# A linear-attention and GEGLU block: the order of its work written by hand, and the same work ordered by a list scheduler inside the kernel

## The chip, the core and the metric

One core of a Trainium2 chip runs the kernel. Its engines each take their own queue in order: PE (TensorE, matrix products), ACT (ScalarE), DVE (VectorE), POOL (GpSimd), and SP (SyncE), which here issues every transfer between the device's memory (DRAM) and the core's working memory (SBUF). Products land in PSUM, eight banks of 128 x 512 numbers. The metric is device time in microseconds (us), the median of three runs; a profiled execution is taken beside them.

## The reference, cut to what matters

```python
x = A_x                                   # 1 x 2048 x 512, float32
xn = layernorm(x)
q, k, v = split(xn @ wqkv)                # 32 heads of 16
phi = lambda t: where(t > 0, t + 1, exp(t)) + 1e-6
kv = einsum("bhsd,bhse->bhde", phi(k), v);  z = sum over s of phi(k)
o = (phi(q) @ kv) / (phi(q) . z + 1e-6)
s = o @ wo
g = silu((gelu(xn @ w_gate) * (xn @ w_up)) @ w_down)    # w_gate, w_up: 512 x 1792
return x + s * g
```

## The kernel before

**Products.** Every large product is made of numbers split in two: a rounded high part (ACT casts it) and the rest (DVE or POOL subtracts). `mm3` (L83) issues high x high, high x low and low x high, so one product of a 128 x 256 by 256 x 512 block is six matmuls of 512 columns. The projections go by a scheme of seven block products where the plain one has eight: a 2 x 2 blocking of the activations (`xt`, and four differences `T`, made on POOL, L180) and of the weights (`tmp`, made on POOL, L376 to L379). The products carry the numbers 1 to 7 (`PRODUCTS`, L24). They gather in three PSUM tiles: X takes 1, 6, 7 and 4, one on top of the other, and is copied out by ACT after 1, 6 and 7 (`saved`, L418: `e1`, `u2`, `u3`); Y takes 2; Z takes 5 and 3. DVE adds a copy and a PSUM tile (`added`, L422) to get the four output blocks: 11 = e1 + Y, 22 = u3 + Z, 21 = X itself, 12 = u2 + Z. So a product on X has to wait until ACT has copied what stands there.

**Stages.** (A) Layer norm (`ln`, L149), transposes on PE (`transp`, L167), splits, and eight rounds (L288) over pairs of token tiles for q and k: products X, Y, Z, then exp (ACT) and sums (DVE) for phi, and `gacc` (L254), which adds xn-transposed times phi(k) into four PSUM banks `gps`. The weights wq and wk are first combined and split into seven slots `kq` (L131). q goes to DRAM (`q_d`), and so do the split activations of the first four rounds (`xh_d`, `xl_d`). (F1) The gated projection for the second half of the tokens: `ffn` (L403) runs 14 "quads" (`quad`, L447), in turn gate and up, each seven products; a gate quad ends in gelu on ACT, an up quad in a product with the gate on POOL (L438) and a split into `hh` (ACT, L441) and `hl` (DVE, L442). After units 0, 1-2 and 3-4, and at the end 5-6, `down` (L502) multiplies by w_down and adds into eight tiles `acc`. (S) The attention output: `GT`, `wv`, `wo` are loaded, `kv` and `M` made, then for each of 16 token tiles a normalisation (POOL L636, DVE L638 to L643), a transpose `ptq`, a split and twelve matmuls `sps`. (F0) `ffn` for the first half of the tokens, with the final sum in `finish` (L697).

**What sets the order.** Under `manual_schedule` (L63) the four engines run their instructions in the order in which the Python code writes them. That order is by hand: inside `quad` the products come as 2, 6, 5, 7, then 1 of the next quad, then 4 and 3; the preparation of a later quad's weights (`prep_w`, L367: four POOL sums, then casts and subtractions of four groups) is dealt out in steps, `bg` (L451), between the products. Stages have pools of their own, opened and closed one after another, and the tiles rotate through few buffers: `raw` two, `tmp` one, `w` four, X two PSUM banks, Y and Z one each.

Of the kernel before, what the change touches and what calls it, by code (L numbers as in the profile page):

```python
# [8 lines left out]
F32 = mybir.dt.float32  # L9
# [5 lines left out]
P = 128  # L15
# [10 lines left out]

@with_exitstack
def kernel(
# [21 lines left out]
    NF = F // P  # L50
    NU = NF // 2
    NP = 8

    def pool(name, bufs=1, **kw):
        return ctx.enter_context(tc.tile_pool(name=name, bufs=bufs, **kw))

    dram = pool("dram", space=bass.MemoryType.DRAM)
    cpool = pool("cpool")
    xf = pool("xf")
    wp = pool("wp")  # L60
    rawp = pool("rawp")

    ctx.enter_context(tc.manual_schedule(engines=ENGINES))  # L63

    q_d = dram.tile([S, D], F32, name="q_d")
    s_d = dram.tile([S // 2, D], F32, name="s_d")
    g_d = dram.tile([P, KT, D], F32, name="g_d")
    xh_d = dram.tile([P, 14, NC], F32, name="xh_d")
    xl_d = dram.tile([P, 14, NC], F32, name="xl_d")

    neg_half = cpool.tile([P, 1], F32, name="neg_half")
    nc.vector.memset(neg_half, -0.5)
    ones = cpool.tile([P, P], F32, name="ones")
    nc.vector.memset(ones, 1.0)
    ident = cpool.tile([P, P], F32, name="ident")
    make_identity(nc, ident)
    zacc = cpool.tile([P, D], F32, name="zacc")
    den_eps = cpool.tile([P, H], F32, name="den_eps")

    XH = xf.tile([P, 14, NC], F32R, name="XH")  # L80
    XL = xf.tile([P, 14, NC], F32R, name="XL")
# [7 lines left out]
    wqkv_k = wqkv.rearrange("(k p) n -> p k n", p=P)  # L89


    with ExitStack() as actx:
        ap = actx.enter_context(tc.tile_pool(name="ap", bufs=1))
        sm = actx.enter_context(tc.tile_pool(name="sm", bufs=2))
        psa = actx.enter_context(tc.tile_pool(name="psa", bufs=1, space=bass.MemoryType.PSUM))

        xs = {}

        def load_x(t):
            xs[t] = ap.tile([P, D], F32, name=f"x{t}", tag="x", bufs=4)  # L100
            nc.sync.dma_start(xs[t], x[t * P:(t + 1) * P, :])

        tokens = [(8 * (n // 4) + n % 4, 8 * (n // 4) + 4 + n % 4) for n in range(NP)]

        warm = psa.tile([P, P], F32, name="warm", tag="X")
        for _ in range(WARM):
            nc.tensor.matmul(warm, ones, ones, start=True, stop=True)


        wk1 = rawp.tile([P, 2, D], F32, name="wk1", tag="raw", bufs=2)  # L110
        wk2 = rawp.tile([P, 2, D], F32, name="wk2", tag="raw", bufs=2)
        wq1 = rawp.tile([P, 2, D], F32, name="wq1", tag="tmp", bufs=1)
        wq2 = ap.tile([P, 2, D], F32, name="wq2", tag="wq2")
        s1 = ap.tile([P, 2, D], F32, name="s1", tag="s1")
        load_x(0)
        nc.sync.dma_start(wk1, wqkv_k[:, 0:2, D:2 * D])
        load_x(4)
        nc.sync.dma_start(wk2, wqkv_k[:, 2:4, D:2 * D])
        nc.sync.dma_start(wq1, wqkv_k[:, 0:2, 0:D])
        nc.sync.dma_start(wq2, wqkv_k[:, 2:4, 0:D])  # L120
        load_x(1)
        load_x(5)

        KQ = [wp.tile([P, 7, D], F32R, name=f"kq{i}", tag="w", bufs=4) for i in range(4)]
        ORDER = [0, 1, 4, 3, 5, 2, 6]

        def kq(slot, lo, k):
            r = 4 * ORDER.index(slot) + 2 * lo + k
            return KQ[r // 7][:, r % 7, :]

        def kq_split(slot, raw):  # L131

            r = 4 * ORDER.index(slot)
            if r // 7 == (r + 1) // 7:
                nc.scalar.copy(KQ[r // 7][:, r % 7:r % 7 + 2, :], raw)
            else:
                for k in range(2):
                    nc.scalar.copy(kq(slot, 0, k), raw[:, k, :])
            both = (r // 7 == (r + 1) // 7) and ((r + 2) // 7 == (r + 3) // 7)
            if both:  # L140
                a, b = KQ[(r + 2) // 7], KQ[r // 7]
                nc.vector.tensor_sub(a[:, (r + 2) % 7:(r + 2) % 7 + 2, :], raw, b[:, r % 7:r % 7 + 2, :])
            else:
                for k in range(2):
                    nc.vector.tensor_sub(kq(slot, 1, k), raw[:, k, :], kq(slot, 0, k))

        lnst, xns = {}, {}

        def ln(t):  # L149
            st = sm.tile([P, 6], F32, name=f"st{t}", tag="st")  # L150
            nc.vector.bn_stats(st, xs[t])
            mv = sm.tile([P, 2], F32, name=f"mv{t}", tag="mv")
            nc.vector.bn_aggr(mv, st)
            ve = sm.tile([P, 1], F32, name=f"ve{t}", tag="ve")
            nc.vector.tensor_scalar_add(ve, mv[:, 1:2], EPS_LN)
            rstd = sm.tile([P, 1], F32, name=f"rstd{t}", tag="rstd")
            nc.gpsimd.tensor_tensor(rstd, ve, neg_half, op=ALU.pow)
            lnst[t] = mv, rstd

        def ln_norm(t):  # L160
            mv, rstd = lnst.pop(t)
            xns[t] = ap.tile([P, D], F32, name=f"xn{t}", tag="xn", bufs=5)
            nc.vector.tensor_scalar(xns[t], xs.pop(t), mv[:, 0:1], rstd, op0=ALU.subtract, op1=ALU.mult)  # L163

        xts = {}

        def transp(n, i):  # L167
            t = tokens[n][i]
            pt = psa.tile([P, KT, P], F32, name=f"pt{t}", tag="pt")
            for k in range(KT):  # L170
                nc.tensor.transpose(pt[:, k, :], xns[t][:, k * P:(k + 1) * P], ident)  # L171
            if i == 0:
                xts[n] = ap.tile([P, 2, KT, P], F32, name=f"xt{n}", tag="xt")
            nc.scalar.copy(xts[n][:, i], pt)

        Ts = {}

        def forms(n):
            xt = xts[n]
            T = Ts[n] = ap.tile([P, 4, 2, P], F32, name=f"T{n}", tag="T")  # L180
            nc.gpsimd.tensor_sub(T[:, 0], xt[:, 1, 0:2], xt[:, 0, 0:2])
            nc.gpsimd.tensor_sub(T[:, 1], xt[:, 1, 2:4], T[:, 0])
            nc.gpsimd.tensor_sub(T[:, 2], xt[:, 1, 2:4], xt[:, 1, 0:2])
            nc.gpsimd.tensor_sub(T[:, 3], xt[:, 0, 2:4], T[:, 1])

        def jsl(n):
            return slice((n % 4) * P, (n % 4 + 1) * P)

        def split_x(n, part):

            src, rows = {
                0: (xts[n][:, 0], slice(0, 4)),
                1: (xts[n][:, 1, 2:4], slice(4, 6)),
                2: (Ts[n].rearrange("p a b c -> p (a b) c") if n in Ts else None, slice(6, 14)),
            }[part]
            nc.scalar.copy(XH[:, rows, jsl(n)], src)
            nc.vector.tensor_sub(XL[:, rows, jsl(n)], src, XH[:, rows, jsl(n)])

        def spill_x(n):
            nc.sync.dma_start(xh_d[:, :, jsl(n)], XH[:, :, jsl(n)].bitcast(F32))  # L200
            nc.sync.dma_start(xl_d[:, :, jsl(n)], XL[:, :, jsl(n)].bitcast(F32))

        def prod(ps, n, i, start):
            ws, xsl = PRODUCTS[i]
            for k in range(2):
                mm3(ps, XH[:, 2 * xsl + k, jsl(n)], XL[:, 2 * xsl + k, jsl(n)],
                    kq(ws, 0, k), kq(ws, 1, k), start and k == 0, k == 1, not start)

        xn_h, xn_l, pk_h, pk_l = {}, {}, {}, {}

        def split_xn(t):
            xn = xns.pop(t)
            xn_h[t] = ap.tile([P, D], F32R, name=f"xnh{t}", tag="xnh", bufs=3)
            xn_l[t] = ap.tile([P, D], F32R, name=f"xnl{t}", tag="xnl", bufs=3)
            nc.scalar.copy(xn_h[t], xn)
            nc.gpsimd.tensor_sub(xn_l[t], xn, xn_h[t])

        def saved(ps, name):
            e = ap.tile([P, D], F32, name=name, tag="e", bufs=4)
            nc.scalar.copy(e, ps)  # L220
            return e

        def added(e, ps, name):
            c = ap.tile([P, D], F32, name=name, tag="c", bufs=3)
            nc.vector.tensor_add(c, e, ps)
            return c


        def phi_exp(v, t, nm):
            r = ap.tile([P, D], F32, name=f"{nm}r{t}", tag="r", bufs=2)  # L230
            nc.scalar.activation(r, v, AF.Relu, scale=-1.0)
            nc.scalar.activation(r, r, AF.Exp, scale=-1.0)
            return r

        def phi_add(v, r, t, nm):

            p0 = ap.tile([P, D], F32, name=f"{nm}p{t}", tag="p", bufs=4)
            nc.vector.scalar_tensor_tensor(p0, v, 0.0, r, op0=ALU.max, op1=ALU.add)
            return p0
# [496 lines left out]
```

## Time and profile before

| | |
|---|---|
| median of 3 runs | 912.86 us (907.66 to 915.66) |
| profiled execution | 914.31 us, its span from first to last instruction 912.6 us |
| busy in the span | PE 706.3 us (77%), DVE 409.3 (45%), ACT 325.4 (36%), POOL 267.1 (29%) |
| mean clock granted to PE | 0.87 of full speed |
| moved by DMA | 68.64 MB, mean 75 GB/s |

Rows of the profile give a line of the kernel, the engine, the operation, output<-input by tile names, the count (x) and busy time; "idle before" is the time the engine stood still just before, and the arrow names the instruction that ended it. PE's matmuls overlap in the pipe, so their listed durations are longer than their spacing; the spacing of their starts is what counts.

### The profile page before, as it was taken

How to read it: one execution, taken by the hardware profiler on the slowest of the kernel's cores; microseconds unless marked ns; L12 is line 12 of the kernel's file. 1: busy time of each engine (PE TensorE's matmuls, PEld its weight loads, DVE VectorE, ACT ScalarE, POOL GpSimd, SP SyncE). 2: the span in 40 equal slices, each digit the busy share in tenths (PEclk: the TensorE clock that was granted, in tenths of full speed). 3: DMA queues.
4: the chain of work that ended last, by engine and by line, in shares of the span. 5: the costliest groups of instructions: out<-in, count | busy, mean ns of one | idle time of the engine just before them, and what ended most of it. 6: DMA issues, size and time to landing. Idle time of an engine off the chain costs nothing.

```text
span 912.6 us, 7661 instructions
## 1 busy us (share of the span) xinstructions
PE 706.3 (77%) x2760; PEld 558.4 (61%) x2760; DVE 409.3 (45%) x608; ACT 325.4 (36%) x560; POOL 267.1 (29%) x277
## 2 busy tenths in 40 slices
PE   3676666697789689778979667787896897789784
PEld 2565555575667468566757545665674685667663
DVE  7655554555343443443333456553424425443333
ACT  4544454465344430333233311124443413331321
POOL 3443433344221321223112224422223212231023
PEclk7887887898789889889988788899898799799888
DMA  5433410003301110110105725323111101200024
GB/s 205 128 123 109 127 47 23 24 24 109 96 26 47 46 47 0 59 57 24 47 0 231 300 91 150 109 76 105 46 46 47 46 1 47 69 1 23 1 88 164
DMA packets 49637, 68.64 MB, mean 75 GB/s; under 512 B 2496, under 2 KB 31168, under 8 KB 49088
## 3 DMA queue, kind: packets, MB, share of 16 engines
q1 hardware_dynamic: 49600, 68.17, 22.8%
q8 instruction: 21, 0.34, 0.2%
q14 instruction: 16, 0.13, 0.0%
HBM read 49.28 MB, written 18.87 MB: 75 GB/s over the span
## 4 chain that ended last, share of the span: by engine, by line
PE 34%; DVE 13%; issue 11%; POOL 10%; ACT 9%; DMA 2%; SPq 0%; POOLq 0%; DVEq 0%; ACTq 0%
POOL c L438 6%; PE FX L85 5%; PE d L87 5%; PE d L85 5%; PE d L86 5%; PE FX L86 4%; PE FX L87 4%; DVE c L424 4%; ACT fu L419 3%; DVE w L383 2%; ACT hh L441 2%; DVE hl L442 2%; POOL u L636 1%; ACT w L382 1%; POOL tmp L377 1%
## 5 line engine op out<-in xcount | busy, mean ns | idle before, releaser
L85 PE MATMUL FX<-XH,w 128*128 128x512 f32 x224 | 111.9, 500 | 89.7 <-ACT fu L419 84.4
L438 POOL TENSOR_TENSOR c<-c,c 128x512 f32<-128x512 f32 x42 | 53.9, 1283 | 264.6 <-DVE c L424 264.6
L85 PEld LDWEIGHTS FX<-XH,w 128*128 128x128 f32 x224 | 53.7, 240 | 115.1 <-ACT fu L419 96.9
L86 PE MATMUL FX<-XL,w 128*128 128x512 f32 x224 | 105.6, 471 | 0.0
L87 PE MATMUL FX<-XH,w 128*128 128x512 f32 x224 | 104.6, 467 | 0.0
L85 PE MATMUL d<-dw,hh 128*128 128x512 f32 x224 | 87.2, 389 | 0.0
L87 PE MATMUL d<-dw,hl 128*128 128x512 f32 x224 | 87.1, 389 | 0.0
L86 PE MATMUL d<-dw,hh 128*128 128x512 f32 x224 | 87.1, 389 | 0.0
L376 POOL TENSOR_TENSOR tmp<-raw 128x256 f32<-128x256 f32 x28 | 22.1, 791 | 176.5 <-DVE w L383 176.5
L441 ACT CAST hh<-c 128x512 fp32r<-128x512 f32 x42 | 26.0, 618 | 127.9 <-POOL c L438 127.9
L442 DVE TENSOR_TENSOR hl<-c,hh 128x512 fp32r<-128x512 f32 x42 | 29.1, 692 | 94.7 <-ACT hh L441 94.7
L424 DVE TENSOR_TENSOR c<-fu,FZ 128x512 f32<-128x512 f32 x56 | 38.4, 686 | 68.9 <-ACT fu L419 51.1
L516 DVE TENSOR_TENSOR acc<-acc,d 128x512 f32<-128x512 f32 x48 | 32.9, 686 | 71.6 <-PE d L87 71.1
L87 PEld LDWEIGHTS FX<-XH,w 128*128 128x128 f32 x224 | 53.2, 237 | 13.9 <-DVE w L383 0.2
L171 PE MATMUL pt<-ident,xn 128*128 128x128 f32 x64 | 13.9, 357 | 61.6 <-DVE xn L163 61.6
L86 PEld LDWEIGHTS FX<-XL,w 128*128 128x128 f32 x224 | 54.3, 243 | 11.6
L383 DVE TENSOR_TENSOR w<-tmp,w 128x512 fp32r<-128x512 f32 x56 | 39.6, 709 | 44.7 <-ACT w L382 44.5
L419 ACT COPY fu<-FX 128x512 f32<-128x512 f32 x56 | 32.5, 581 | 56.7 <-PE FX L87 56.7
L171 PEld LDWEIGHTS pt<-ident,xn 128*128 128x128 f32 x64 | 10.1, 185 | 65.8 <-issue 61.2
L85 PE MATMUL FZ<-XH,w 128*128 128x512 f32 x112 | 45.8, 409 | 5.0 <-DVE c L424 5.0
L383 DVE TENSOR_TENSOR w<-raw,w 128x512 fp32r<-128x512 f32 (+1 forms) x56 | 35.4, 672 | 27.4 <-ACT w L382 27.4
L87 PEld LDWEIGHTS d<-dw,hl 128*128 128x128 f32 x224 | 42.1, 188 | 8.8
(153 smaller groups left out, 1573.2 us busy)
## 6 DMA issues: line engine op xcount, KB each, us to landing
raw<-in_B_w_gate SPq DMA_DIRECT2D x14, 512.0 KB, 3.8
raw<-in_B_w_up SPq DMA_DIRECT2D x14, 512.0 KB, 3.8
draw<-in_B_w_down SPq DMA_DIRECT2D x14, 512.0 KB, 3.5
x<-in_A_x SPq DMA_DIRECT2D x16, 256.0 KB, 3.1
q_d<-qp SPq DMA_DIRECT2D x16, 256.0 KB, 2.0
q<-q_d SPq DMA_DIRECT2D x16, 256.0 KB, 2.6
xh_d<-XH SPq DMA_DIRECT2D x4, 896.0 KB, 4.9
xl_d<-XL SPq DMA_DIRECT2D x4, 896.0 KB, 7.1
```

Source lines behind the costliest of these rows:

```text
L85: nc.tensor.matmul(ps, wh, mh, start=start, stop=False, skip_group_check=on)
L86: nc.tensor.matmul(ps, wh, ml, start=False, stop=False, skip_group_check=on)
L87: nc.tensor.matmul(ps, wl, mh, start=False, stop=stop, skip_group_check=on)
L171: nc.tensor.transpose(pt[:, k, :], xns[t][:, k * P:(k + 1) * P], ident)
L376: nc.gpsimd.tensor_add(tmp[:, 0:2], a21, a22)
L383: nc.vector.tensor_sub(w[:, 1, rows], src, w[:, 0, rows])
L419: nc.scalar.copy(e, ps)
L424: nc.vector.tensor_add(c, e, ps)
L438: (eng or nc.vector).tensor_mul(h, other, src)
L441: nc.scalar.copy(hh, h)
L442: nc.vector.tensor_sub(hl, h, hh)
L516: nc.vector.tensor_add(acc[p, j], acc[p, j], ps)
```

## The change

The same instructions are kept, but for a few (PE's counted instructions stay as they were), and the code no longer writes them in order. Each operation is now *stated*: `do(engine, cost, function, output, inputs...)` enters it in a `Plan` with what it reads and writes. `Plan.order` gets a written order for PE (`pe_keys`), works back from it how late each other operation may end, and then deals out all operations engine by engine in simulated time: the ready operation that is needed soonest goes first, an engine may be kept free for a more urgent one, and PE may run up to 6 us ahead in its written list. The costs are constants in the code.

```diff
+class Plan:
+    AHEAD = 6.0
+    HOP = {"PE": 0.3, "ACT": 0.15, "DVE": 0.15, "POOL": 0.15, "SP": 0.0}
...
+                t = max(free[e], min(o.ready for o in c))
+                o = min((o for o in c if o.ready <= t), key=lambda o: o.late)
+                end = t + o.cost
+                for u in c:
+                    if u.ready > t and u.ready < end and u.late < min(end, o.late):
+                        o, t = u, u.ready
...
+def act(n):
+    return 0.17 + 0.00086 * n
+def dve(n):
+    return 0.16 + 0.00104 * n
+def pool(n):
+    return 0.18 + 0.00215 * n
...
+    for q in range(base, base + NQ):
+        more = q + 1 < base + NQ
+        if q == base:
+            keys += [("F", q, 1), ("F", q, 2)]
+        keys += [("F", q, 6), ("F", q, 5), ("F", q, 7)]
+        if more:
+            keys += [("F", q + 1, 1), ("F", q + 1, 2)]
+        keys += [("F", q, 4), ("F", q, 3)]
...
+    mt = tile_in("xf", "h", [P, 14, NC], F32, "mstuff", 8)
...
+    order = [t for a, b in zip(range(8, 16), range(8)) for t in (a, b)]
...
+    for o in plan.order(pe_keys):
+        o.fn()
```

With this come: (1) a quad's written order is 6, 5, 7, then 1 and 2 of the next quad, then 4, 3; Z has two banks. (2) In stage A the first three rounds do only products 1 and 2 at first (`EARLY = 3`), with a fresh X later to which DVE adds e1; `gacc` lags by a round and is placed between products; three of the seven `kq` subtractions go to POOL. (3) All stages share one set of buffers, so one stage's work may start while the last one still runs. (4) GT, wv, wo, zb and kv lie in the place of XH (`mstuff`), so they are loaded after F1's last product, and XH comes back from DRAM in seven pieces once the last reader of `mstuff` is done. (5) Stage S alternates tiles of the second and the first half. (6) The last tile of all ends in two halves.

What stands where now is shown at three places. PE, from the first instruction after the warm-up; pt0 is the transpose of token tile 0, X0 and Y0 are round 0's products 1 and 2, and a product's further rows are left out. Before:

```order
L171 MATMUL pt0_147<-ident_80,xn0_143 128x128 x4
L171 MATMUL pt4_169<-ident_80,xn4_162 128x128 x4
L171 MATMUL pt1_225<-ident_80,xn1_202 128x128 x4
L85 MATMUL X0_232<-kq0_127,XH_87 128x512
...
L85 MATMUL Y0_245<-kq0_127,XH_87 128x512
```

In the change:

```order
L416 MATMUL pt0_153<-ident_90,xn0_148 128x128 x4
L282 MATMUL X0_181<-kq0_137,Xh0_168 128x512
...
L282 MATMUL Y0_194<-kq0_137,Xh0_168 128x512
...
L416 MATMUL pt1_216<-ident_90,xn1_209 128x128 x4
L416 MATMUL pt2_230<-ident_90,xn2_225 128x128 x4
L282 MATMUL X1_242<-kq0_137,Xh0_168 128x512
```

The first product stood behind three transposes and now stands behind one.

ACT, in quad 3 (the up quad of unit 1): fu2 and fu3 are the copies of X after products 6 and 7, fe1 the copy after product 1 of the next quad, hh the casts of the gated values. Before:

```order
L414 CAST dw1_1_1899<-draw1_1_1653 128x1024
L441 CAST hh1_1_11_1922<-c11_3_1915 128x512
L419 COPY fu2_3_1932<-FX3_1797 128x512
L382 CAST w5_1906<-raw5_1749 128x512
L382 CAST w5_1906<-raw5_1749 128x256
L419 COPY fu3_3_1951<-FX3_1797 128x512
L441 CAST hh1_1_22_1956<-c22_3_1953 128x512
L419 COPY fe1_4_1967<-FX4_1960 128x512
```

In the change:

```order
L268 CAST dwh1_2_2004<-draw1_2_1899 128x1024
L268 COPY fu2_3_2015<-FX3_1854 128x512
L268 COPY acc1_7_2017<-d1_0_7_1989 128x512
L268 COPY fu3_3_2034<-FX3_1854 128x512
L268 COPY fe1_4_2045<-FX4_2027 128x512
L268 CAST hh22_3_2056<-h22_3_2036 128x512
L687 ACTIVATE g11_4_2054<-g11_4_2054 128x512
```

The three copies of X moved ahead of the casts `hh`, which wait for POOL.

SP, around the end of F1 and in stage S (q8 is a tile of q, raw16 a weight tile of F0). Before:

```order
L561 DMA XL_88<-xl_d_75 128x7168
L560 DMA XH_87<-xh_d_74 128x7168
L578 DMA GT2_3222<-g_d_73 128x2048
L365 DMA raw16_3206<-in_B_w_gate 128x4x256
L579 DMA wv_3223<-in_A_wqkv 128x4x512
L580 DMA wo_sb_3224<-in_A_wo 128x4x512
```

In the change, the end of F1 and, after the dots, some ten tiles of S later:

```order
L264 DMA Xl0_174<-xl_d_87 128x1024
L264 DMA q9_3135<-q_d_83 128x512
L264 DMA mstuff_3141<-g_d_85 128x512
L264 DMA mstuff_3141<-in_A_wqkv 128x4x512
L264 DMA mstuff_3141<-g_d_85 128x512 x3
L264 DMA mstuff_3141<-in_A_wo 128x4x512
...
L264 DMA out_y<-acc1_4_1970 128x512
L264 DMA Xh2_3796<-xh_d_86 128x1024
L264 DMA s_d_84<-so4_3783 128x512
L264 DMA Xh2_3796<-xh_d_86 128x1024 x6
```

The loads for `kv` and `M` moved ahead of the return of XH, which is now in pieces and later.

More of the change, by code (lines that the diff above doesn't have):

```diff
@@ L67 @@
[L67 to L78, printed above, removed]
@@ new lines, with tile_in, get, ring @@
+    gens = {}
+    def tile_in(pool_name, unit, shape, dtype, name, parts=1):
+        gen = gens[pool_name, unit] = Gen(gens.get((pool_name, unit)))
+        kept = []
+        def get():
+            if not kept:
+                kept.append(pools[pool_name].tile(shape, dtype, name=name, tag=f"{pool_name}{unit}", bufs=1))
+            return kept[0]
+        return View([Res() for _ in range(parts)], get, gen)
+    count = {}
+    def ring(tag, places):
+        n = count[tag] = count.get(tag, -1) + 1
+        return places[n % len(places)]
@@ new lines, with split_xn, saved, added @@
+    xn_s, pk_s = {}, {}
+    def split_xn(t):
+        h = U("xnh", range(9, 12), f"xnh{t}", F32R)
+        lo = U("xnl", range(12, 15), f"xnl{t}", F32R)
+        copy("ACT", h, xns[t], D, "xnh")
+        tt("POOL", "sub", lo, xns[t], h, D, "xnl")
+        xn_s[t] = h, lo
+    def saved(ps, name):
+        e = U("e", range(15, 19), name)
+        copy("ACT", e, ps, D, name)
+        return e
+    def added(e, ps, name, places=("c", range(19, 22))):
+        c = U(*places, name)
+        tt("DVE", "add", c, e, ps, D, name)
+        return c
@@ L352 @@
+    GT = []
+    for c in range(KT):
+        g = U("p", range(24, 28), f"GTa{c}")
+        copy("DVE" if c % 2 else "ACT", g, gps[c], D, "GT")
+        dma(g_d(c, (slice(None), c)), g, 256)
     gate_k = w_gate.rearrange("(k p) n -> p k n", p=P)
@@ new lines, in fprod, with run, prep_d @@
+        g = GROUP_OF[a]
+        wv = w.part(w.res[g:g + 1], (slice(None), slice(None), slice(2 * a, 2 * a + 2)))
+        xv = [xrows(hl, b, b + 1) for hl in "hl"]
+        def run(o, w, xh, xl):
+            for k in range(2):
+                mm3(o, w[:, 0, k], w[:, 1, k], xh[:, k], xl[:, k], start and k == 0, k == 1, not start)
+        do("PE", 1.37, run, ps, wv, *xv, key=("F", q, i), name="fprod")
+    acc, hs, gs, dws = {}, {}, {}, {}
+    def prep_d(p, u):
+        raw = D2(0, f"draw{p}_{u}")
+        dma(raw, ext(down_f[:, 2 * u:2 * u + 2, :]), 512)
+        k = ring("dw", [0, 1])
+        dh, dl = D2(1 + 2 * k, f"dwh{p}_{u}", F32R), D2(2 + 2 * k, f"dwl{p}_{u}", F32R)
+        split(dh, dl, raw, 2 * D, "dw")
+        dws[p, u] = dh, dl
@@ L601, with make_mask @@
+    for c in range(KT):
+        dma(GT.part(GT.res[c:c + 1], (slice(None), c)), g_d(c, (slice(None), c)), 256)
+    dma(wv, ext(wqkv_k[:, :, 2 * D:3 * D]), 1024)
+    dma(wo_sb, ext(wo.rearrange("(k p) n -> p k n", p=P)), 1024)
+    ones_r = const("ones_r", [P, P], F32R)
+    copy("ACT", ones_r, ones, P)
+    mask2 = const("mask2", [P, P])
+    def make_mask(o):
+        mask = o.rearrange("p (b d) -> p b d", d=DH)
         nc.gpsimd.memset(mask, 1.0)
@@ L675 @@
[L675 to L709 removed]
+    do("POOL", 1.5, make_mask, mask2)
@@ new lines @@
+    M = []
+    for nm in ("M_hi", "M_lo"):
+        sl = w_next[0] % 4
+        w_next[0] += 1
+        M.append(tile_in("wp", sl, [P, KT, D], F32R, nm, KT))
+    for g in range(KT):
+        pm = bank([0, 1, 2, 4][g], f"pm{g}")
+        do("PE", 0.9, lambda o, a, b, g=g: nc.tensor.matmul(o, a[:, g, :], b[:, g, :], start=True, stop=True),
+           pm, kv4, wo_sb, key=("m", g))
+        split(M[0].part(M[0].res[g:g + 1], (slice(None), g)), M[1].part(M[1].res[g:g + 1], (slice(None), g)), pm, D, "M")
@@ new lines, in finish0 @@
+    def finish0(p, j):
+        n = 2 if j == 7 else 1
+        sr, xr = U("fe", FE, f"fs{j}"), U("fc", FC, f"fx{j}")
+        dma(sr, s_d(j, slice(j * P, (j + 1) * P)), 256)
+        dma(xr, ext(x[j * P:(j + 1) * P, :]), 256)
+        w = D // n
+        silu(p, j, n)
+        for i in range(n):
+            cl = (slice(None), slice(i * w, (i + 1) * w))
+            do("DVE", dve(w), lambda o, a: nc.vector.tensor_mul(o, o, a), sr[cl], acc[p, j][cl])
+            eng = nc.vector if n == 2 and i else nc.gpsimd
+            do("DVE" if n == 2 and i else "POOL", pool(w), lambda o, a, eng=eng: eng.tensor_add(o, o, a), sr[cl], xr[cl])
+            dma(ext(out[j * P:(j + 1) * P, i * w:(i + 1) * w]), sr[cl], 256 // n)
```

1133 lines of the change are left out of this document (606 added, 527 removed).

## The prediction, made before the result was seen

> **What bounds the kernel now.** I first read the stages, cut where PE's stage changes: to the first product, A, F1, S with F1's last down, F0, and the last down with the tail.
>
> ```profile
> 0.00:27.00 27.00, 7.02 (x30) 6.19 (x30) 20.06 (x27) 10.84 (x14) 9.97 (x15) 0.69 0.61 204
> 27.00:219.80 192.80, 144.37 (x584) 115.42 (x585) 103.77 (x151) 94.09 (x162) 77.83 (x77) 0.86 0.22 70
> 219.80:488.40 268.60, 220.85 (x828) 173.82 (x829) 106.17 (x154) 93.90 (x167) 65.47 (x72) 0.87 0.15 45
> 488.40:614.86 126.46, 95.54 (x395) 74.19 (x394) 66.40 (x115) 27.92 (x48) 42.90 (x40) 0.88 0.50 173
> 614.86:877.70 262.84, 216.80 (x830) 171.16 (x829) 101.07 (x146) 91.69 (x162) 59.33 (x64) 0.89 0.13 39
> 877.70:912.60 34.90, 21.74 (x96) 17.65 (x94) 11.84 (x19) 6.95 (x10) 11.55 (x9) 0.88 0.45 150
> ```
>
> Behind the length stand PE, PE's loads, DVE, ACT and POOL, busy time and count, then PE's granted clock. No other engine comes near PE, and DMA is idle most of the time. But PE's busy time is no floor. F1's last down is 96 matmuls with no wait between them:
>
> ```profile
> 488.40 0.40 PE L85 MATMUL d<-dw,hh 128*128 128x512 f32 x1
> 509.97 0.39 PE L87 MATMUL d<-dw,hl 128*128 128x512 f32 x1
> 490.00:510.00 20.00, 20.00 (x90) 16.52 (x88) 5.41 (x8) 6.33 (x9) 4.04 (x5) 1.00 0.82 349
> ```
>
> (509.97 - 488.40) / 95 = 0.227 us each at full clock, so a product of six takes 1.363 us. F1's 828 matmuls would take 188.0 us by that, and take 268.6. What lies between, the waits tell (waiting, waited for, us, times, longest), and a stretch of an up quad:
>
> ```profile
> PE FX L85 <- ACT fu L419: 84.4, 28, 4.8
> PE pt L171 <- DVE xn L163: 61.6, 8, 15.7
> ACT hh L441 <- POOL c L438: 127.9, 42, 4.9
> 397.53 0.72 POOL L379 TENSOR_TENSOR tmp<-raw,tmp 128x256 f32<-128x256 f32 x1
> 398.21 1.26 POOL L438 TENSOR_TENSOR c<-c,c 128x512 f32<-128x512 f32 x1
> 399.51 0.62 ACT L441 CAST hh<-c 128x512 fp32r<-128x512 f32 x1 [4.88 <-POOL c L438]
> 400.03 0.58 ACT L419 COPY fu<-FX 128x512 f32<-128x512 f32 x1
> 400.66 0.80 PE L85 MATMUL FX<-XH,w 128*128 128x512 f32 x1 [4.80 <-ACT fu L419]
> 401.26 0.63 PE L86 MATMUL FX<-XL,w 128*128 128x512 f32 x1
> 401.68 0.63 PE L87 MATMUL FX<-XH,w 128*128 128x512 f32 x1
> ```
>
> The copy `fu` that PE needs is ready to run, but stands in ACT's queue behind `hh`, which waits for POOL's product, which waits behind four POOL sums for a later quad. PE stands 4.80 us. And then it runs slow: starts 0.42 us apart (401.26, 401.68) where 0.227 is normal, until here:
>
> ```profile
> 406.30 0.39 PE L86 MATMUL FX<-XL,w 128*128 128x512 f32 x1
> ```
>
> The 13 matmuls from 400.66 to 406.30 take 5.64 us instead of 2.95. So a stall of 3 to 5 us costs some 2.7 us more in a cold clock. The kernel is bound by the order in ACT's and POOL's queues, a stall per quad: 84.4 us directly, and the mean clock of 0.87 with it.
>
> **The change, part by part.** The sum is made against the profiled span, 912.6 us; the execution's own time is 1.7 us more, and the median of the runs, 912.86, lies within 0.3 us of the span.
>
> *Start.* PE's first product waited for three transposes and nearly all of the weights' preparation:
>
> ```profile
> 27.05 1.09 PE L171 MATMUL pt<-ident,xn 128*128 128x128 f32 x4 [15.73 <-DVE xn L163]
> 27.79 0.78 PE L85 MATMUL X<-kq,XH 128*128 128x512 f32 x1
> 24.28 2.34 POOL L281 TENSOR_TENSOR wk<-wk,wk 128x1024 f32<-128x1024 f32 x1
> wq<-in_A_wqkv SPq DMA_DIRECT2D x2, 512.0 KB, 6.7
> L424 DVE TENSOR_TENSOR c<-fu,FZ 128x512 f32<-128x512 f32 x56 | 38.4, 686 | 68.9 <-ACT fu L419 51.1 <-PE FZ L87 17.8
> ```
>
> Now three rounds' products 1 and 2 and their `gacc` come first. The next thing, product 6 of round 0, needs the combined weights. Ahead of it stand on DVE thirty operations of 512 columns (0.69 each by L424: 20.7) from about 4 us on; on POOL five of 512 (1.26), two of 1024 (2.34), four of 256 (0.72) and a few short ones, some 16 us, from wq's landing near 10 us on. Both end near 26, and they hinder each other (below), so I put product 6 at 33 us. Left for PE in A are then 50 products (68.2), 52 `gacc` of three (35.4) and ten transposes:
>
> ```profile
> 608.92 0.63 PE L652 MATMUL ptq<-ident,pn 128*128 128x128 f32 x4 [0.68 <-DVE pn L643]
> 609.30 0.48 PE L85 MATMUL sps<-M_hi,pqTh 128*128 128x512 f32 x1
> ```
>
> at 0.38, 3.8 together: 107.4, to 140. To this comes what PE still waits. Least: nothing. Most: what A loses now, 192.8 less 524 x 0.227 and 15 x 0.38, that is 68. I take 16, near the lower end, because 46 of the 61.6 us on xn fall in the rounds and go with the lagging `gacc` and the earlier layer norm, and above zero because DVE, busy 123.8 us in A and given nine additions more (6.2) and three subtractions less, will have hardly more room than PE. A ends at 156 us, not 219.8: 64 gained.
>
> *F1 and F0.* Products and downs stay: 188.0 each. The copies of X leave the shadow of `hh` (the ACT rows shown). Product 7 follows 6 with only 5 between, 1.363 us; the round trip over ACT is 0.58 for the copy and some 0.3 around it, so it is hidden if ACT is free, and short by up to 0.1 if a cast of 0.62 has just begun. Placing 2 of the next quad behind 1 gives product 4 two products of cover (2.7) instead of one. ACT and DVE are at 94 and 106 of 188 then, so all is covered on the whole. Remaining wait per half: least zero (490:510 shows a stretch without any), most what stands now, 81. I take 12, some 0.85 us per quad, by what DVE and POOL do to each other:
>
> ```profile
> 593.94 1.28 POOL L636 TENSOR_TENSOR u<-q,zb 128x512 f32<-128x512 f32 x1 [2.42 <-DVE den L638]
> 594.51 1.26 DVE L643 SCALAR_TENSOR_TENSOR pn<-q,r 128x512 f32<-128x512 f32 x1
> L442 DVE TENSOR_TENSOR hl<-c,hh 128x512 fp32r<-128x512 f32 x42 | 29.1, 692 | 94.7 <-ACT hh L441 94.7
> L383 DVE TENSOR_TENSOR w<-tmp,w 128x512 fp32r<-128x512 f32 x56 | 39.6, 709 | 44.7 <-ACT w L382 44.5
> ```
>
> DVE's `pn` took 1.26 us instead of 0.69 and ended 0.55 after POOL's `u` (595.22): it stood until POOL was done. A wait of that kind once or twice a quad makes the 12. The costs stated in the code have no such term. Stalls this short leave the clock as it is:
>
> ```profile
> 378.16 0.50 PE L85 MATMUL FZ<-XH,w 128*128 128x512 f32 x1 [0.94 <-DVE c L424]
> 378.50 0.39 PE L86 MATMUL FZ<-XL,w 128*128 128x512 f32 x1
> 378.73 0.40 PE L87 MATMUL FZ<-XH,w 128*128 128x512 f32 x1
> ```
>
> 0.23 us apart after 0.94 us of standing. Gain: (268.6 - 200) + (262.84 - 200) = 131.
>
> *S.* Floor: the down's 21.8, 192 `sps` 43.6, 16 transposes 6.1, `pz`, `pkv` and `pm` some 7: 78.5. Per tile DVE's work is den, pn and pqTl near 0.69 each, two short ones, and in every second tile a product: about 3.1 us, as much as PE's 12 x 0.227 + 0.38 = 3.1.
>
> ```profile
> 583.00:614.86 31.86, 24.86 (x111) 19.25 (x110) 17.56 (x30) 7.53 (x13) 9.93 (x10) 0.95 0.28 91
> wv<-in_A_wqkv SPq DMA_DIRECT2D x1, 1024.0 KB, 6.5
> XH<-xh_d SPq DMA_DIRECT2D x1, 3584.0 KB, 20.6
> ```
>
> The 111 instructions here are seven tiles, 4.6 us each. Between 3.1 and 4.6 I take 3.5: 56 for 16. GT and wv may now land only after F1's last product: some 2 us of issue and 6.5 to land, against 8.0 of down and `pz` on PE ahead of `pkv`; a wait of 2, in which `pm` and the rest of the down stand behind `pkv` on PE, and the normalisation goes on, since it waits for `pz` alone. XH's return I cost at nothing: it is issued with six tiles to go, 21 us, and took 20.6 while XL came beside it; if that cover is gone, it is up to 20 us, and F0 is late by it. Together 21.8 + 7 + 2 + 56 and 4 for the chains at both ends: 91, not 126.5. Gain 35.
>
> *End.* PE's last matmul is followed by 13 us, for the last s_d tiles are loaded late:
>
> ```profile
> 899.05 0.39 PE L87 MATMUL d<-dw,hl 128*128 128x512 f32 x1
> 905.40 0.69 DVE L700 TENSOR_TENSOR sr<-acc,sr 128x512 f32<-128x512 f32 x1 [4.21 <-DMA sr<-s_d]
> ```
>
> With three places for them, loads ahead of the last tiles and halves at the end I put 6.5: gain 6.7.
>
> Sum: 156 + 200 + 91 + 200 + 21.8 + 6.5 = **675 us**, a quarter less. The unhidden work alone (33 + 107 + 188 + 79 + 188 + 22 + 5) gives 622 as a floor. The chain of sums behind the raw weights, and the SP rows in another order, I cost at nothing; that is the last rival.
>
> **The rivals.** *DVE and POOL block each other*, chance 0.22. In FFN the DVE operations that read two SBUF tiles are, per half, 28 + 28 of w, 21 + 7 of `hl` and 7 of dw. If all of some 90 stand for half a POOL operation (0.5 us) and half of that reaches PE, it is 22 per half instead of the 12; if each holds PE for its whole half, 45. I put 32, 20 more than the forecast. In A, where POOL's 88 us and DVE's 124 must pass in 156, I put 14 more, in S 5: 675 + 14 + 2 x 20 + 5 = 734. For it: the pair of rows above. Against it: in F1 both together need less than 172 of 188 even if nothing overlapped. The Trainium skill, "SBUF — State Buffer", section "SBUF: two separate sides", says that GpSimd and a VectorE instruction with two SBUF inputs hold the shared ports as an exclusive lock, the loser blocked for the whole instruction; the trace agrees, with 1.26 against 0.69 us. By that rule every such meeting counts in full, and this rival's time is the one to expect, not the forecast's.
>
> *The stalls are a latency and not an order*, 0.10: PE waits for ACT's copies as before, because X is one tile and the trip is long. Then F1 and F0 stay, and only start, A, S and the end gain: 912.6 - 64 - 35 - 7 = 807. Against it: `fu` needed 0.58 us and stood behind `hh` for nearly 5.
>
> *Slower, 0.04*: the weights' chain falls behind. One queue issues every transfer, two raw buffers and one tmp remain, and in the new order a load can stand behind a store that waits.
>
> ```profile
> raw<-in_B_w_gate SPq DMA_DIRECT2D x14, 512.0 KB, 3.8
> ```
>
> If every quad had to wait for its own load (3.8), four sums (2.9), two casts (1.2) and a subtraction (0.7), 8.6 us in all, and 2.7 in the cold clock behind it, it would be 28 x 11.3 = 316: 991. It decides from 8.5 us per quad on, (912.6 - 675) / 28. Against it: four w tiles let preparation run two quads ahead, and the downs (21.8 us without a product) let it catch up.
>
> **How the numbers follow.** Forecast 0.64, its own range 640 to 715; blocking 0.22, 715 to 750; latency 0.10; slower 0.04. The range 640 to 750 takes in the first two and leaves 0.14 and a little out. One per cent is about what a measurement here can tell from no change: faster by more 0.96 (the first three), within it 0.01, slower 0.03, these two out of the last.
>
> **What would show it.** Right: first product before 14 us, product 6 of round 0 near 33; F1's first product near 150; PE's waits on `fu` under 1 us and its clock above 0.95 from there on; F1 and F0 near 200 us each; 3.5 us per tile in S; 6 to 7 us after the last matmul. Wrong: DVE subtractions of w and `hl` well over 0.75 us on average and PE waiting for them (blocking), PE's waits on copies of X of 3 us at a cold clock (latency), PE waiting for w after a late load (the chain).

## The result and the profile after

The changed kernel takes 662.16 us (median of 4 runs, 661.48 to 663.49), the kernel before 914.23 in the same session (907.66 to 915.66): a ratio of 0.7255, 95% interval 0.7216 to 0.7293. The forecast was 675 us, 13 too high; the time lies inside the range of 640 to 750. The profiled execution of the changed kernel spans 660.8 us at a mean granted clock of 0.981 (before: 912.6 at 0.870). One execution of experiment 3 took 906.25 us at a granted clock of 0.651, where its other three had 0.971 to 0.979; it is left out of that experiment's numbers.

The stages of the changed kernel, in the columns of the first view of the prediction. They are cut at the first product, the first product of F1, the last of F1, the first of F0 and the last of F0:

```profile
0.00:13.87 13.87, 4.95 (x26) 4.52 (x26) 4.45 (x12) 5.62 (x10) 3.81 (x12) 0.78 0.72 246
13.87:160.47 146.60, 132.03 (x564) 102.56 (x565) 127.09 (x180) 96.11 (x170) 102.13 (x91) 0.96 0.36 108
160.47:354.66 194.19, 194.14 (x857) 160.44 (x856) 117.63 (x159) 97.59 (x171) 76.00 (x77) 1.00 0.25 79
354.66:441.69 87.03, 83.31 (x393) 66.92 (x392) 65.21 (x112) 26.31 (x45) 36.67 (x30) 0.98 0.66 221
441.69:630.74 189.05, 188.95 (x833) 155.82 (x831) 106.05 (x143) 91.91 (x160) 64.39 (x64) 1.00 0.16 48
630.74:660.80 30.06, 21.24 (x94) 17.27 (x92) 15.09 (x22) 7.75 (x13) 11.42 (x9) 0.93 0.59 192
```

In both halves of the FFN PE is busy for all but 0.1 us, at full clock. The third stage still holds the last 24 matmuls of `gacc` (163.19 to 168.63, 5.4 us). With that given back to A, the terms of the sum read:

| term | forecast | measured |
|---|---|---|
| A | 156 | 165.9 |
| F1 | 200 | 188.8 |
| S, with F1's last down | 91 | 87.0 |
| F0 | 200 | 189.0 |
| last down and tail | 28.3 | 30.1 |
| together | 675.3 | 660.8 |

PE's waits (waiting, waited for, us, times, longest), and ACT's longest group of waits for PE's X:

```profile
PE X L282 <- ACT Xh L268: 7.0, 1, 7.0
PE pt L416 <- DVE xn L405: 5.3, 4, 1.9
PE gps L283 <- DVE pkl L490: 3.1, 3, 1.6
ACT fu L268 <- PE FX L284: 35.8, 42, 2.1
```

PE waits for `fu` no more; the direction has turned, and ACT stands ready for PE's X. What was feared of DVE and POOL is there all the same. The groups, with mean ns of one:

```profile
L714 POOL TENSOR_TENSOR h<-h,g 128x512 f32<-128x512 f32 x42 | 61.9, 1474 | 176.9 <-DVE h L274 176.9
L274 DVE TENSOR_TENSOR hl<-h,hh 128x512 fp32r<-128x512 f32 x56 | 53.5, 973 | 3.5 <-ACT hh L268 3.3
L274 DVE TENSOR_TENSOR w<-tmp,w 128x512 fp32r<-128x512 f32 x56 | 43.1, 776 | 4.4 <-ACT w L268 3.9
```

`hl` went from 692 to 973 ns, w from 709 to 776. A stretch of an up quad shows both things at once, from the time line of each engine:

```profile
237.63 1.68 POOL L714 TENSOR_TENSOR h<-h,g 128x512 f32<-128x512 f32 x1 [2.08 <-DVE h L274]
237.47 2.39 DVE L274 TENSOR_TENSOR hl<-h,hh 128x512 fp32r<-128x512 f32 x2
238.27 0.59 ACT L268 COPY fu<-FX 128x512 f32<-128x512 f32 x1 [0.26 <-PE FX L284]
239.16 0.39 PE L284 MATMUL FZ<-Xh,w 128*128 128x512 f32 x1
239.39 0.39 PE L282 MATMUL FX<-Xh,w 128*128 128x512 f32 x1
```

Two `hl` take 2.39 us instead of 1.3 because POOL's `h` lies between them; the copy `fu` goes out 0.26 us after ACT came free, and PE goes from product 5 to product 7 at its 0.23 us spacing.

### The profile page after: what moved, and what is told of

The parts are those of the page before. It is cut to its first block, busy times and chain, and to the rows that moved or that the text cites. A ratio compares the mean times of both kernels' runs of the same rounds, so it can differ in the third digit from the quotient of the medians.

```text
span 660.8 us, 7812 instructions
## 1 busy us (share of the span) xinstructions
PE 624.6 (95%) x2760; PEld 507.5 (77%) x2760; DVE 435.5 (66%) x626; ACT 325.3 (49%) x566; POOL 294.4 (45%) x282
## 4 chain that ended last, share of the span: by engine, by line
PE 82%; DVE 7%; DMA 4%; ACT 2%; issue 2%; POOL 1%; SPq 1%; DVEq 0%; POOLq 0%; ACTq 0%
PE FX L282 8%; PE FX L284 8%; PE FX L283 8%; PE d L282 6%; PE d L283 6%; PE d L284 6%; PE FZ L284 4%; PE FZ L282 4%; PE FZ L283 4%; PE sps L284 2%; PE sps L282 2%; PE sps L283 2%; PE FY L282 2%; PE FY L284 2%; PE FY L283 2%
## 5 line engine op out<-in xcount | busy, mean ns | idle before, releaser
L714 POOL TENSOR_TENSOR h<-h,g 128x512 f32<-128x512 f32 x42 | 61.9, 1474 | 176.9 <-DVE h L274 176.9
L282 PE MATMUL d<-dwh,hh 128*128 128x512 f32 x224 | 87.7, 391 | 0.0
L282 PE MATMUL FX<-Xh,w 128*128 128x512 f32 x224 | 87.5, 390 | 0.2
L284 PE MATMUL FX<-Xh,w 128*128 128x512 f32 x224 | 87.2, 389 | 0.0
L283 PE MATMUL FX<-Xl,w 128*128 128x512 f32 x224 | 87.2, 389 | 0.0
L284 PE MATMUL d<-dwh,hl 128*128 128x512 f32 x224 | 87.2, 389 | 0.0
L283 PE MATMUL d<-dwl,hh 128*128 128x512 f32 x224 | 87.2, 389 | 0.0
L274 DVE TENSOR_TENSOR hl<-h,hh 128x512 fp32r<-128x512 f32 x56 | 53.5, 973 | 3.5 <-ACT hh L268 3.3
L282 PEld LDWEIGHTS FX<-Xh,w 128*128 128x128 f32 x224 | 42.0, 188 | 10.1 <-ACT fu L268 1.4
L283 PEld LDWEIGHTS d<-dwl,hh 128*128 128x128 f32 x224 | 42.1, 188 | 9.0 <-issue 0.2
L284 PEld LDWEIGHTS FX<-Xh,w 128*128 128x128 f32 x224 | 42.1, 188 | 8.8
L282 PE MATMUL FZ<-Xh,w 128*128 128x512 f32 x112 | 43.6, 389 | 0.0
L284 PE MATMUL FZ<-Xh,w 128*128 128x512 f32 x112 | 43.6, 389 | 0.0
```

What stands on the lines that cost most here:

```text
L274: do(eng, c, lambda o, p, q: getattr(e, f"tensor_{op}")(o, p, q), dst, a, b, name=name)
L282: nc.tensor.matmul(ps, wh, mh, start=start, stop=False, skip_group_check=on)
L283: nc.tensor.matmul(ps, wh, ml, start=False, stop=False, skip_group_check=on)
L284: nc.tensor.matmul(ps, wl, mh, start=False, stop=stop, skip_group_check=on)
L714: do("POOL", pool(NC), lambda o, i: nc.gpsimd.tensor_mul(o, o, i), h, g, name="h")
```

## The experiments

The theory was: PE stood because copies of X were queued behind operations that waited for POOL; the cure is the order in ACT's and POOL's queues. Against it stood a latency of the trip over ACT, the other order of the products, the early products of A, and the blocking of DVE and POOL.

**1. The casts `hh`, and with them the subtractions `hl`, written later in the kernel before; nothing else.**

```diff
+            def cut():
...
+                nc.scalar.copy(hh, h)
+                nc.vector.tensor_sub(hl, h, hh)
...
+            late.append(cut)
...
             c22 = added(u3, Z, f"c22_{q}", tag)
+            cuts()
...
                 emit_h(u, 21, X, gs.pop((u, 21)), None)
+                cuts()
...
```

> The kernel before, with one edit: the casts `hh` and subtractions `hl` of the gated values are written later in the queues (those of 11 and of the last 12 behind the copy `u3`, those of 22 and 21 behind product 4). Order theory (the copies of X stood behind casts that wait for POOL): PE's waits on `fu` fall from 84.4 us to under 25, F1 and F0 become 50 to 70 us shorter each with the warmer clock, the whole 770 to 840 us. Latency theory (the trip over ACT is too long for one X tile): `fu` stays above 70 us and the time between 890 and 915.

The time is 787.71 us, ratio 0.8641 (0.8597 to 0.8686). PE's waits on `fu`, and the two halves of its FFN:

```profile
PE FX L85 <- ACT fu L419: 8.1, 14, 0.7
220.91:426.15 205.24, 193.91 (x829) 156.56 (x830) 108.70 (x152) 91.78 (x166) 74.19 (x72) 0.98 0.19 59
551.33:751.15 199.82, 191.06 (x830) 154.55 (x829) 103.43 (x144) 89.74 (x161) 67.82 (x64) 1.00 0.17 52
```

The order theory holds, within its range. The latency is refuted, for with the same X tiles, the same trip and the same order of products PE waits 8.1 us instead of 84.4. The halves became 63.4 and 63.0 us shorter, 126.4, of which the waits are 76.3. The other 50, some 1.8 us per stall, are put down to the time in which PE ran slowly after one: the clock of the halves rose from 0.87 and 0.89 to 0.98 and 1.00, and PE's busy time for the same matmuls fell from 437.7 to 385.0 us.

**2. The old order of the products, in the changed kernel.**

```diff
-                keys += [("F", q + 1, 1), ("F", q + 1, 2)]
+                keys.append(("F", q + 1, 1))
             keys += [("F", q, 4), ("F", q, 3)]
...
+            if more:
+                keys.append(("F", q + 1, 2))
```

> The changed kernel with the written PE order of a quad as it was: product 2 of the next quad goes behind product 3, not behind product 1; all queues are still planned. Queue theory (what mattered is the order on ACT, DVE and POOL): 660 to 668 us. Theory that the other order of the seven products carries the gain: product 4 has one product of cover (1.36 us) for its copy, it waits 0.3 to 1.5 us in each of 28 quads, 670 to 705 us.

662.0 us, ratio 0.7268 (0.7236 to 0.7300): no difference. "Another order of the seven products" carries nothing; one product of cover is enough once ACT is free.

**3. One early round instead of three.** `EARLY = 1`.

> The changed kernel with one round instead of three that does products 1 and 2 at first. If PE has nothing else to do while the combined weights are made, four products (5.5 us), their `gacc` (some 4 us) and two transposes move behind: F1 begins 5 to 12 us later, 667 to 675 us. If stage A is bound by DVE and POOL instead of PE, the later rounds take the same time and it stays at 660 to 664 us.

662.03 us, ratio 0.7255 (0.7204 to 0.7307): the time stays, as the second expectation had it. Product 6 of round 0 and the first product of F1:

```profile
31.70 0.39 PE L282 MATMUL X0b<-kq,Xh 128*128 128x512 f32 x1
158.20 0.39 PE L282 MATMUL FX<-Xh,w 128*128 128x512 f32 x1
```

Product 6 comes 7.6 us earlier than with three rounds (39.29), F1 2.3 us earlier, and S, 90.1 us instead of 87.0, gives it back. The early products bring nothing in the time; that what they fill on PE is lost by the combined weights coming later is a reading of these rows, not shown apart.

**4. No urgency in the plan.**

```diff
+        for i, o in enumerate(self.ops):
+            if o.eng != "PE":
+                o.late = float(i)
...
-                for u in c:
+                for u in (c if e == "PE" else ()):
```

> The changed kernel with another rule for ACT, DVE, POOL and SP: among the operations that are ready the one stated first goes, and no engine is kept free for a more urgent one; PE as it is. Theory that readiness is enough (nothing stands in a queue ahead of what it waits for): 662 to 675 us. Theory that the urgency is what keeps PE fed: the copies of X and the weights come late again, PE waits 1 us or more in most quads and its clock falls with it, 690 to 780 us.

678.89 us, ratio 0.7452 (0.7416 to 0.7487), above the one range and below the other: both expectations missed. The place of the loss tells more:

```profile
PE pt L419 <- DVE xn L408: 14.8, 2, 13.4
23.71 0.79 PE L285 MATMUL X<-kq,Xh 128*128 128x512 f32 x1 [3.34 <-ACT Xh L271]
172.80:370.52 197.72, 194.91 (x856) 160.27 (x857) 106.22 (x154) 95.76 (x170) 71.45 (x78) 1.00 0.25 77
457.64:647.30 189.66, 189.03 (x833) 155.77 (x831) 97.77 (x143) 90.12 (x160) 61.52 (x64) 1.00 0.15 45
```

The weights, stated first, go ahead of the layer norm: the first product comes at 23.7 instead of 13.9 us, F1 12.3 later. In the FFN the plan without urgency loses 3.5 and 0.6 us. There readiness is nearly all, as the first experiment says too.

**5. DVE against POOL, measured alone.** Each stretch is sixteen DVE and eight POOL operations of 128 x 512.

```diff
+    nc.vector.tensor_add(dv[i], gate, b)     # two SBUF tiles
+    nc.vector.tensor_add(dv[i], gate, pt)    # SBUF and PSUM
+    nc.vector.tensor_scalar(dv[i], gate, 2.0, 1.0, op0=ALU.mult, op1=ALU.add)
+    nc.gpsimd.tensor_add(po[i], gate, b)
```

> The disputed cost by itself; the reference's computation is left out. Sixteen DVE and eight POOL operations of 128 x 512, first each kind alone, then at the same time: DVE adds of two SBUF tiles with POOL adds, DVE adds of an SBUF and a PSUM tile with POOL adds, DVE operations with one SBUF input with POOL adds. Theory that DVE and POOL exclude each other: alone 0.62 us (DVE, 16 starts) and 1.26 us (POOL); together the stretch is the sum, 9.9 + 10.1 = 20 us, with two SBUF tiles; with a PSUM tile it is the longer of the two, 10 to 11 us. Theory that they only slow each other a little: 10 to 13 us in every case. For one SBUF input the rows of stage A (0.98 us on average, 0.54 at least) speak for the sum as well.

The time line gives each run of equal operations one row: start, length, count. Alone (the first two), then together in pairs, and the one-input operation alone:

```profile
4.10 9.72 DVE L65 TENSOR_TENSOR dv<-gate,b 128x512 f32<-128x512 f32 x16 [4.10 <-DMA b<-in_A_x]
15.90 9.79 POOL L77 TENSOR_TENSOR po<-gate,b 128x512 f32<-128x512 f32 x8 [0.73 <-ACT gate L61]
27.80 18.24 DVE L65 TENSOR_TENSOR dv<-gate,b 128x512 f32<-128x512 f32 x16 [1.39 <-ACT gate L61]
27.91 13.37 POOL L77 TENSOR_TENSOR po<-gate,b 128x512 f32<-128x512 f32 x8 [2.22 <-ACT gate L61]
47.45 9.66 DVE L69 TENSOR_TENSOR dv<-gate,pt 128x512 f32<-128x512 f32 x16 [1.41 <-ACT gate L61]
47.56 9.86 POOL L77 TENSOR_TENSOR po<-gate,b 128x512 f32<-128x512 f32 x8 [6.28 <-ACT gate L61]
58.75 13.98 DVE L73 TENSOR_SCALAR dv<-gate 128x512 f32<-128x512 f32 x16 [1.64 <-ACT gate L61]
58.85 11.24 POOL L77 TENSOR_TENSOR po<-gate,b 128x512 f32<-128x512 f32 x8 [1.44 <-ACT gate L61]
74.13 5.46 DVE L73 TENSOR_SCALAR dv<-gate 128x512 f32<-128x512 f32 x16 [1.41 <-ACT gate L61]
```

With two SBUF tiles DVE takes 18.24 us, near the sum (19.5). With a PSUM tile it takes 9.66, and POOL 9.86 in the same stretch, as alone (9.79): neither holds the other up. With one SBUF input it takes 13.98, for 5.46 alone; the sum would be 15.3. In these runs the two engines exclude each other, unless DVE reads PSUM. The Trainium skill, "SBUF — State Buffer", section "SBUF: two separate sides", states such an exclusive lock for a VectorE instruction with two SBUF inputs, or in a 2-port performance mode, against GpSimd. The two-tile run agrees but for an overlap of 1.3 us in 19.5; whether the operation with one input is in such a mode no run here shows.

**6. Three times the sums of the weights, in the changed kernel.**

```diff
+        for _ in range(3):
+            tt("POOL", "add", t(0), a21, a22, 256, "S1")
...
```

> The changed kernel with each of the four POOL sums of a quad's weights done three times over (the same numbers again): 80 us more for POOL in each half of the FFN. In F1 POOL is busy some 82 us of 189, DVE with two SBUF inputs some 55. Theory that the two exclude each other: 82 + 80 + 55 = 217 us have to pass in 189, each half becomes 25 to 45 us longer, the whole 710 to 760 us. Theory that they do not: POOL has 162 us of work in 189, all behind the four w tiles, each half stays within 5 us, 660 to 672 us.

692.05 us, ratio 0.7582 (0.7546 to 0.7617). The halves (the first again with the last `gacc`), the wait that came back, and what ACT waited for:

```profile
165.17:374.87 209.70, 200.75 (x857) 163.36 (x855) 133.65 (x159) 97.35 (x172) 171.37 (x189) 0.98 0.24 73
463.65:661.34 197.69, 190.88 (x833) 155.30 (x832) 119.56 (x143) 90.21 (x160) 138.67 (x152) 1.00 0.15 46
PE FX L282 <- ACT fu L268: 15.6, 10, 2.7
ACT w L268 <- POOL tmp L274: 87.0, 41, 13.5
ACT hh L268 <- POOL h L715: 42.3, 30, 3.9
```

The halves are 15.5 and 8.6 us longer: between the two expectations, and both missed. POOL's busy time in these two stretches more than doubled, from 140.4 to 310.0 us, and the halves lost 24.1 us. What came back is a wait for `fu`, and behind it ACT waited for POOL: 87.0 us for its sums, 5.6 in the changed kernel, and 42.3 for its `h`, 20.9 there. So the run has two causes in one, POOL's longer queue and the blocking (DVE's busy time in the halves rose from 223.7 to 253.2 us for the same 302 instructions), and does not tell them apart. In the changed kernel itself, unforced, the blocking costs PE no more than the 1 us that each half exceeds 188.0. That a count of 217 us in 189 would lengthen a half by the difference did not hold. F1 itself began 4.7 us later than at 160.47, and S took 1.8 more, which is the rest of the 30 but for the tail, 0.6 shorter.

**7. `xnl` on DVE instead of POOL, and 8. no `zacc` on POOL.** Both are in A, where DVE and POOL are fullest.

```diff
-        tt("POOL", "sub", lo, xns[t], h, D, "xnl")
+        tt("DVE", "sub", lo, xns[t], h, D, "xnl")
```

> The changed kernel with the 16 subtractions `xnl` of stage A given to DVE instead of POOL, nothing else. DVE is busy 136 us of A's 166, POOL 107. Theory that A is bound by what DVE and POOL exclude of each other (POOL's 93 us of work and some 66 of DVE's with two SBUF inputs, 159 in all): 16 x (1.26 - 0.62) = 10 us less of it, DVE's other operations get shorter, F1 begins 3 to 8 us earlier, 654 to 660 us. Theory that DVE's own queue binds: 16 x 0.62 = 10 us more in it, F1 begins 3 to 10 us later, 664 to 673 us.

662.65 us, ratio 0.7272 (0.7230 to 0.7314); F1 began at 160.28 (160.47): neither range. From the first product to F1, DVE ran 191 instructions instead of 180 in no more busy time (125.6 us against 127.1). The two effects may have cancelled; the run does not tell the theories apart.

```diff
-        do("POOL", pool(D), lambda o, i: nc.gpsimd.tensor_add(o, o, i), zacc, p0, name="zacc")
```

> The changed kernel without POOL's 16 adds `zacc` of stage A (the sum of phi(k) over the tokens is left out, so the normalisation is another). They are 22 us of POOL's work, and PE waits for none of them before stage S. Theory that POOL's work in A costs PE time by standing in DVE's way: DVE is busy 6 us or more less before 160 us with the same instructions, F1 begins 3 to 8 us earlier, 654 to 660 us. Theory that A is late for its own chains (DVE's work, the order at the start): DVE's busy time falls but F1 begins within 2 us of 160.5, 660 to 663 us.

660.98 us, ratio 0.7242 (0.7213 to 0.7272). From the first product to F1:

```profile
14.41:158.87 144.46, 131.78 (x565) 103.29 (x565) 118.72 (x181) 95.98 (x171) 81.47 (x76) 0.96 0.36 110
```

DVE's 181 instructions take 118.7 us; in the changed kernel 180 took 127.1. So POOL's adds cost DVE some 8 us, but F1 begins only 1.6 us earlier, as the second theory had it. The blocking is not what makes A late, or not by itself.

**9. Truer landing times for the first loads, 10. with places for the last tiles, 11. with the exclusion in the plan.**

```diff
+            started[0] += kb
+            lat = max(lat, 1.3 + started[0] / 270.0)
```

> The changed kernel with truer landing times stated for the first ten loads (bytes so far at 270 GB/s), so that on ACT the cast of wq does not stand ahead of the first round's X any more. Theory that the 7.0 us for which PE waits for `Xh` at the start is a cause of the late stage A: first product at 8 us, product 6 of round 0 near 34 instead of 39, F1 begins 3 to 6 us earlier, 656 to 660 us. Theory that something behind it binds (DVE and POOL until 100 us): the first product is early, F1 begins within 1 us of where it did, 661 to 663 us.

660.66 us, ratio 0.7239 (0.7199 to 0.7279). The first product came at 12.06 (the first x tile was now loaded later), product 6 at 37.96, F1 at 158.71, 1.8 us earlier. That lies between the two expectations, closer to "something behind it binds".

```diff
-        sr, xr = U("fe", FE, f"fs{j}"), U("fc", FC, f"fx{j}")
+        sr, xr = U("fs", [6, 7, 8, 9, 34, 35], f"fs{j}"), U("fs2", [0, 1, 2, 3, 4, 5], f"fx{j}")
```

> A try for a faster version: the changed kernel with the landing times of the first loads stated by the bytes ahead of them (the first x tile stays first) and six places each for the last tiles of s_d and x, so that their loads go out during F0. First product near 10 us instead of 13.9, F1 2 to 5 us earlier; after the last matmul 6 to 7 us instead of 9.2: 654 to 658 us. If the start is taken up by DVE and POOL behind it, only the tail gains: 659 us.

660.7 us, ratio 0.7236 (0.7206 to 0.7266). The last product with s_d, in the changed kernel and in this one:

```profile
655.69 0.87 DVE L935 TENSOR_TENSOR fs<-fs,acc 128x256 f32<-128x256 f32 x2 [1.09 <-DMA fs<-s_d]
```

```profile
654.74 0.76 DVE L942 TENSOR_TENSOR fs<-fs,acc 128x256 f32<-128x256 f32 x2 [0.54 <-ACT acc L766]
```

It waits for ACT now and no longer for a load, and the end comes 6.5 us after the last matmul (653.1 to 659.6), not 9.2 (651.6 to 660.8). But S took 1.3 us more and the start gained nothing (first product 13.56, F1 160.38), so the expected 654 to 658 us was missed; the time is also 1.7 us above the 659 expected of the tail alone.

```diff
+                if o.port:
+                    t = max(t, port)
```

> The run with loads and tail, and the plan now lets no POOL operation and no DVE operation on SBUF alone run at the same time (one port that both take). Theory that the missing term made the plan's order wrong where DVE and POOL are full: stage A ends 3 to 8 us earlier than without the term, 648 to 655 us. Theory that the engines sort it out by themselves, since each queue's order hardly changes: within 2 us of the run without the term.

659.34 us, ratio 0.7220 (0.7186 to 0.7254): the lowest of all, 1.4 us under the run without the term, not to be told from it or from the changed kernel. F1 began later, at 162.48. The term is worth nothing here.

**12. The tiles of S in the old order.** `order = list(range(8, 16)) + list(range(8))`.

> The changed kernel with stage S's tiles in the order of before: the eight of the second half, then the eight of the first. If taking the halves in turn made the tiles faster (a second-half tile has one DVE product more), the first eight take 0.3 to 0.6 us more each and the whole is 663 to 668 us. If the tiles gained by the order in the queues (PE waited 21.0 us for `pn` before), S keeps its 3.3 us per tile: 660 to 663 us. XH's return begins at the same tile or one later either way.

662.7 us, ratio 0.7262 (0.7232 to 0.7291); S takes 87.06 us, as in the changed kernel (87.03). Taking the halves in turn is not what made S shorter.

## Why the prediction was right, and where its terms were off

**The main step holds, and is shown.** The stalls were an order, and they and the cold clock behind them were to go. Half of the 251.8 us comes from this alone: 126.4 of the FFN's 153.6 with the casts `hh` and subtractions `hl` moved and nothing else (experiment 1). The price of the clock was somewhat high: 2.7 us per stall taken from one, 1.8 on average. In the FFN of the kernel before, every stall of 3.1 us or more left PE slow behind it, no single one of less than 1 us did, and 1.88 us did once (at 286.40) and once not (675.97). Experiment 1 keeps 14 waits on `fu` of up to 0.7 us, at clocks of 0.98 and 1.00.

**That the sum came so near is in part luck.** A and the tail took 11.7 us more than forecast, F1, S and F0 26.2 less; a good part of the errors cancelled.

**F1 and F0 were the largest error, 11 us each.** The spacing of the matmuls was right: 828 of them would take 188.0 us, the halves take 188.8 and 189.0. The 12 us of remaining wait per half, "by what DVE and POOL do to each other", were mis-sized; they are 1. The blocking is as strong as feared (`hl` 973 ns), but it falls on DVE, 118 of 194 us busy, and stops there: in both halves PE has no listed wait for DVE. The forecast priced a wait of DVE as if PE had to share it. It took 170 us more of POOL's busy time to get waits on `fu` back (experiment 6). With the casts moved alone the halves come to 205.2 and 199.8 us (experiment 1), about the forecast's 200. The rest of the change gave the last 27 us; the order of the products is not it (experiment 2), the urgency is some 4 us of it (experiment 4), and the other parts were not tried alone.

**A was 10 us longer than forecast.** What PE loses after product 6 was right in size: 126.6 us less 50 products (68.2), 56 `gacc` (38.1) and eleven transposes (4.2) leaves 16.1, forecast 16. Of it 9.3 us are listed waits, all but 0.7 for results of DVE, as forecast; the rest is slower spacing. As 16 was picked between 0 and 68, the exact hit is luck. What failed is the time of product 6, 39.3 instead of 33, and with it 8 `gacc` ahead of it instead of 12. In rows of the changed kernel:

```profile
11.55 0.62 ACT L268 CAST kq<-wq 128x512 fp32r<-128x512 f32 x1 [4.23 <-DMA wq<-in_A_wqkv]
13.20 0.62 ACT L268 CAST Xh<-xt 128x512 fp32r<-128x512 f32 x1
13.85 0.69 DVE L274 TENSOR_TENSOR Xl<-xt,Xh 128x512 fp32r<-128x512 f32 x1 [4.91 <-ACT Xh L268]
29.96 3.46 DVE L274 TENSOR_TENSOR wk<-s,wk 128x512 f32<-128x512 f32 x2
30.36 2.52 POOL L274 TENSOR_TENSOR kq<-wq,kq 128x1024 fp32r<-128x1024 f32 x1
35.36 1.91 POOL L274 TENSOR_TENSOR T<-xt 128x256 f32<-128x256 f32 x1 [1.44 <-ACT xt L268]
```

My list had DVE at work from 4 us on without a gap. In fact ACT's queue held a cast of wq ahead of the first X, and DVE stood 4.91 us: the very fault that the change removes in the FFN, made again by a stated landing time that was too short. Then DVE's two subtractions `wk` take 3.46 us instead of 1.3 beside POOL's 2.52, and the first `T` 1.91 instead of 0.72. Experiment 3 shows the rest of it: without the early rounds' work ahead, product 6 comes at 31.7. But an earlier product 6 moved F1 by 2.3 us at most. Which work holds A between 14 and 100 us, where DVE is busy 78 of 86, stays open (from 100 us on PE is busy 60.4 of 60.5): six kernels, those of experiments 3 and 7 to 11, start F1 between 2.3 us earlier and 2.0 later, none the 10 that the forecast missed. Against the kernel before, A still gained 54 us, and PE's waits for `xn` fell from 61.6 to 5.3, as forecast; but no run moved the layer norm or the lag of `gacc` alone, so this part is read from the profiles and not shown by an experiment.

**S was 4 us shorter,** mostly the tile at 3.27 us instead of 3.5 (16 tiles from 389.31 to 441.69). Neither the early products of A nor the alternation in S carries a gain (experiments 3 and 12); which part of the new queues makes S's tiles faster was not tried alone. **The tail** was 9.2 us instead of 6.5, because the last loads of s_d still came late; with places for them it is 6.5 (experiment 10).

**The rivals.** Latency falls with experiment 1. The weights' chain kept up: PE waits for no w in the FFN. Of the blocking rival the mechanism is real (experiment 5) and its price is not: it would have made 734. One of its signs came, `hl` well over 750 ns; the other, PE waiting for it, did not. By the rule of the Trainium skill, "SBUF — State Buffer", section "SBUF: two separate sides", each meeting counts in full. That is nearly right for DVE's time (18.24 of 19.5 us in experiment 5) and says nothing of who waits for DVE.

## What to carry to other kernels

Read a stall not only by what PE waits for, but by what stands ahead of that in its engine's queue: a ready copy behind a cast that waits for a third engine costs its wait and then a cold clock. Move those casts first; they were half of a 252 us gain, and the scheduler with its other edits made the rest. And price a blocked engine by its own slack: DVE, busy 118 of 194 us, had `hl` stretched from 692 to 973 ns, and PE lost about 1 us per half.

## What was not expected of the hardware

For the blocking the prediction counted only DVE operations with two SBUF inputs. An operation with a single one (0.34 us per 128 x 512) is held up by eight POOL adds as much as one with two: 5.46 us alone and 13.98 beside them, against 9.72 and 18.24, which is 8.5 us more in both. In stage A the layer norm's `xn` shows it, 0.98 us on average where it takes 0.54 undisturbed. With a PSUM operand there is no effect to be seen: sixteen adds take 9.66 us beside POOL, where those of two SBUF tiles take 9.72 alone. So an addition that can take one source from PSUM is free of POOL here.
